# Attention plus gMLP on one core: attention output loaded four token tiles at a time, two raw weight blocks and one maxima row on other queues

## The chip, the cores and the metric

The kernel is one program on one core of a Trainium2 chip. The metric is the device time of one execution in microseconds (us), the median over the runs; a single execution is also recorded by the hardware profiler, and all views of the profile come from that one. In what follows TensorE is PE, its weight loads PEld, VectorE is DVE, ScalarE is ACT, GpSimd is POOL and SyncE is SP. SP computes nothing here: it issues transfers (DMAs), and a few are issued by ACT.

## The reference, cut to what matters

```python
def attention(x, wqkv, wo):                       # S 2048, D 640, 32 heads of 20, window 256
    q, k, v = split(x @ wqkv)
    scores = q @ k^T * 20 ** -0.5                 # key at most 255 tokens back, none ahead
    return (softmax(scores) @ v) @ wo

def gmlp(x, w_in, w_sp, b_sp, w_out):             # F 1728, half of it 864
    z = gelu(x @ w_in)
    z1, z2 = z[:, :864], layernorm(z[:, 864:])
    return (z1 * (w_sp @ z2 + b_sp)) @ w_out      # w_sp mixes the 2048 tokens

h = x + attention(layernorm(x), wqkv, wo)
h2 = h + gmlp(layernorm(h), w_in, w_sp, b_sp, w_out)
```

All is fp32. The two layernorms of 640 have no weights.

## The kernel before, in words

The 2048 tokens are 16 tiles of 128. A large product of fp32 operands is made of three: each operand is split into a high part (`hi`, a rounded copy, mostly made by ACT) and a low part (`lo`, the remainder, mostly made by DVE), and hi x hi, hi x lo and lo x hi are summed (`gemm`, line 98, is the loop for the output projection). Operands that DVE and ACT split are therefore always wanted by PE a little later.

**Stages.** Up to about 232 us come the first layernorm, the transposes and the projections to q, k and v; q and k are stored in DRAM (`qk_d`). From about 234 to 458 us runs attention. From 458 to about 525 us the attention output is multiplied by `wo`, and from 517 us on, mixed with its later tiles, z = h x w_in begins. The rest is the gMLP.

**Attention.** The heads are 8 groups of 4. A unit is one group and one tile of 128 keys, 128 units in all. The loop over s (line 823) does three things in each round. `max_item` works 16 units ahead: products of q and k for a running maximum per query (L344, then DVE's reduction L356). `score_item` makes the scores of unit s with the maximum already subtracted in the product (L410), takes the exponential on ACT (L413, four instructions of one head each per unit) and has POOL zero what lies outside the window (L415, L418); the result is a tile `pt`, of which there are four. `pv_item` multiplies the unit two rounds back by v (L438). Finished sums go through tiles `ot` to DRAM (`o_d`, L455), transposed: 32 rows per head, 20 of them values and the next the sum of the exponentials.

The maxima get into the score product as three extra rows of the operand in a group's slot: `max_rows` (L359 to L379) splits them in three on POOL, transposes them by a product, lets DVE copy them to `mt` (L376) and stores `mt` by DMA into rows 120 to 122 of the slot (L378). It does so twice per group, first for half 0 (b = 0), then for half 1 (b = 1, read from unit 8 of the group on). For group 0 the DMA is issued by ACT, for the other groups by SP. Rows of q and k for the next groups are loaded by SP (L311).

**The attention output's way back.** `load_o(j)` (L146 to L164) loads two tiles (256 tokens) into a ring of three buffers in `m1`: `load_tiles` issues five DMAs (L152), one for each chunk of 128 of the 640 rows, and one more brings the sums, each spread over the 20 rows of its head. For j = 0 the sums come straight from `o_d` and DVE takes their reciprocal over the whole buffer (L162). For the others they are read from `r_d` (`load_rs`, L158), where reciprocals already stand: `inverse_sums(c)` loads the sums of 512 tokens as a 128 x 128 tile `inv` (L389), some rounds later takes the reciprocal on DVE (L392) and has SP store it in `r_d` (L393). Tokens 512c and up are c, so r_d's second row block (c = 1) serves tiles 4 to 7.

For each tile `norm_o` (L168, DVE) multiplies by the reciprocals, `split_o` makes the two parts (`xb`; high by ACT or, at the start, by DVE L174, low by DVE L177), and `proj_o` runs the 30 products of L98. Then DVE adds x (tile `xh`, loaded by L144) and reduces, ACT squares and normalises, and the result goes to DRAM by ACT (L1537) and SP.

`load_win1` (L193, L194) loads two raw blocks of w_in, 442 KB each, into `wraw`. `win1_prep` (L937 to L962) turns w_in into the seven pieces `zl` with their parts, the high one by ACT (L897), the low one and the differences by DVE (L882). PE uses them at L1088.

**What sets the order.** Up to the end of attention (L859) the order of instructions on PE, ACT and DVE is that of the code, and so is SP's. Behind that, `wo_tile(i)` (from L1514) writes tile i's work together with three steps of `win1_prep` and, from tile 8 on, four steps of z, and a scheduler with its own model of times puts the instructions of each engine in order; each engine then runs its list strictly in that order. Before, `proj_early(s)` places by hand: x tiles 0 and 1 at s = 113, load 0 at 117, load 1 at 121, load 2 and the two raw blocks at 126, x tiles 2 and 3 and the last sums at 127. Loads 3 to 7 are called in `wo_tile` of tiles 0, 2, 4, 6 and 8.

In the function that follows these lines are the ones to find: L152, L158 and L162 (loads and first reciprocal), L168, L174, L177 (norm and split), L194 (raw blocks), L378 (maxima row).

Of the kernel before, what the change touches and what calls it, by code (L numbers as in the profile page):

```python
# [8 lines left out]
F32 = mybir.dt.float32  # L9
# [7 lines left out]
P = 128  # L17
S = 2048
D = 640
H = 32  # L20
DH = 20
NT = S // P
# [14 lines left out]
def block_kernel(ctx, tc, x, wqk, wv, wo, w_in, wsp, bsp, w_out, out):  # L37
# [66 lines left out]
    mem = {}  # L104

    def open_early(pl):
        mem["m1"] = pl.tile([P, 6 * D + 6 * P], F32, name="m1")
        mem["xh"] = [pl.tile([P, D], F32, name=f"xh{i}") for i in range(4)]
        mem["inv"] = [pl.tile([P, P], F32, name=f"inv{i}") for i in range(2)]
        mem["wraw"] = pl.tile([P, 2, 2, HF], F32, name="wraw")  # L110
# [23 lines left out]
    def m1(lo, *shape):  # L134
        return view(mem["m1"], lo, *shape)
# [9 lines left out]

    def load_o(j):  # L146

        t = slice(2 * j * P, (2 * j + 2) * P)
        ot, rs = m1(j % 3 * 2 * D, KD, 2 * P), m1(6 * D + j % 3 * 2 * P, 2 * P)
        def load_tiles():  # L150
            for k in range(KD):
                nc.sync.dma_start(ot[:, k], o_d[:, 4 * k:4 * k + 4, t])  # L152

        for i in range(2):
            ots[2 * j + i] = (ot[:, :, i * P:(i + 1) * P], rs[:, i * P:(i + 1) * P])

        def load_rs(base=r_d[:, t], step=S):
            nc.sync.dma_start(rs, bass.AP(tensor=base.tensor, offset=base.offset, ap=[[step, H], [0, 4], [1, 2 * P]]))  # L158

        def load_sums():  # L160
            load_rs(o_d[:, DH, t], 32 * S)
            return lambda: nc.vector.reciprocal(out=rs, in_=rs)  # L162

        return load_tiles, load_rs, load_sums  # L164

    def norm_o(i, eng):
        ot, rs = ots[i]
        eng.tensor_tensor(out=ot, in0=ot, in1=rs[:, None, :].to_broadcast([P, KD, P]), op=OP.mult)  # L168
# [22 lines left out]
            nc.vector.tensor_tensor(out=wo_part(1, k), in0=wo_raw(k), in1=wo_part(0, k).bitcast(F32), op=OP.subtract)  # L191

    def load_win1(b):  # L193
        nc.sync.dma_start(mem["wraw"][:, b], w_in[2 * b * P:(2 * b + 1) * P, :FH].rearrange("k (h c) -> k h c", h=2))  # L194

    def proj_early(s):

        k, odd = divmod(s - 98, 2)
        if 0 <= k < KD and not odd:
            nc.sync.dma_start(wo_raw(k), wo_d[k])  # L200
        if 111 <= s < 111 + 2 * KD:
            split_wo(s - 111)
        if s == 113:
            for i in range(2):
                load_x2(i)
        if s == 117:
            tiles, _, sums = load_o(0)
            mem["invert"] = sums()
            tiles()
        if s == 121:  # L210
            tiles, mem["rs"], _ = load_o(1)
            tiles()
            mem["invert"]()
        if s == 122:
            mem["rs"]()
            norm_o(0, nc.vector)
        if s == 123:
            split_o(0, True)
        if s == 124:
            norm_o(1, nc.vector)  # L220
        if s == 125:
            split_o(1, True)
        if s == 126:
            for b in range(2):
                load_win1(b)
            tiles, mem["rs"], _ = load_o(2)
            tiles()
        if s == 127:
            for i in (2, 3):
                load_x2(i)  # L230
            mem["rs"]()


    with ExitStack() as ab:
# [124 lines left out]
        def max_rows(g, b):  # L359


            n, cols, st = (40, 32)[b], m_cols.pop(b), slot_w[g % 3]
            m3 = tmp2.tile([P, 3, n], BF16, tag="m3", bufs=1, name=f"m3_{g}_{b}")
            mr = tmp2.tile([P, n], F32, tag="mr", bufs=1, name=f"mr{g}_{b}")
            nc.gpsimd.tensor_copy(out=m3[:, 0], in_=cols)
            nc.gpsimd.tensor_tensor(out=mr, in0=cols, in1=m3[:, 0], op=OP.subtract)
            nc.gpsimd.tensor_copy(out=m3[:, 1], in_=mr)
            nc.gpsimd.tensor_tensor(out=m3[:, 2], in0=mr, in1=m3[:, 1], op=OP.subtract)
            if b == 0:
                nc.gpsimd.tensor_copy(out=m_cols[1].rearrange("p (h r) -> p h r", h=4)[:, :, :2],  # L370
                                      in_=cols.rearrange("p (h r) -> p h r", h=4)[:, :, 8:])
            yield
            ps = s1_tile()[:3 * n, :P]
            nc.tensor.matmul(ps, m3.rearrange("p a c -> p (a c)"), minus, start=True, stop=True)
            mt = tmp2.tile([3 * n, P], BF16, tag="mt", bufs=1, name=f"mt{g}_{b}")
            nc.vector.tensor_copy(mt, ps)  # L376
            yield
            (nc.sync if g else nc.scalar).dma_start(st[b][0][120:123], mt.bitcast(F32))  # L378
            yield  # L379

        p_tiles, pv_tiles, inverse, put_later = {}, {}, [], []
# [1123 lines left out]
    def run(n):  # L1505
        for f in later.pop(n, []):
            f()
        if 0 <= n < len(steps):
            steps[n][0]()
            steps[n][1]()  # L1510
# [3 lines left out]
    def wo_tile(i):  # L1514
        if 1 < i + 1 < NT:
            split_o(i + 1, i == 1)
        if i % 2 == 0 and i + 6 < NT:
            for f in load_o(i // 2 + 3)[:2]:
                f()
        if i + 2 < NT:  # L1520
            norm_o(i + 2, nc.vector)
        for n in (4,) if i == 0 else (i + 4,) if i + 4 < NT else ():
            load_x2(n)
        if i < LAG:
            run(i - LAG)
        if i < 2:
            for _ in inverse[2 + i]:
                pass
        ps = pre_ps[i] if i < 2 else proj_o(i, acc_tile(i))
        xt = hs.pop(i)  # L1530
        h3 = xt.rearrange("p (a b) -> p a b", a=2)
        mv = const.tile([P, 5], F32, tag="mv", bufs=3, name=f"mvc{i}")
        nc.vector.tensor_tensor_reduce(out=h3, in0=ps[:, :, :HD], in1=h3, scale=1.0, scalar=0.0,
                                       op0=OP.add, op1=OP.add, accum_out=mv[:, 0:1])
        nc.vector.tensor_scalar(out=mv[:, 1:2], in0=mv[:, 0:1], scalar1=-1.0 / D, scalar2=None, op0=OP.mult)
        nc.scalar.activation(hn(i), xt, AF.Square, bias=mv[:, 1:2], accum_out=mv[:, 2:3])
        nc.scalar.dma_start(h_d[i], xt)  # L1537
        nc.vector.tensor_scalar(out=mv[:, 2:3], in0=mv[:, 2:3], scalar1=1.0 / D, scalar2=EPS, op0=OP.mult, op1=OP.add)
        nc.gpsimd.tensor_tensor(out=mv[:, 3:4], in0=mv[:, 2:3], in1=half, op=OP.pow)
        if i in (2, 5):  # L1540
            nc.vector.tensor_scalar(out=ones[:, i // 5:i // 5 + 1], in0=mv[:, 3:4], scalar1=1.0, scalar2=1.0,
                                    op0=OP.max, op1=OP.min)
        nc.vector.tensor_tensor(out=mv[:, 4:5], in0=mv[:, 1:2], in1=mv[:, 3:4], op=OP.mult)
        nc.scalar.activation(hn(i), xt, AF.Identity, scale=mv[:, 3:4], bias=mv[:, 4:5])
        store_hn(i)
        for _ in range(3):
            next(w1, None)
# [62 lines left out]
```

## Time and profile before

| | |
|---|---|
| median of 3 runs | 1094.03 us (1093.27 to 1096.68) |
| the profiled execution's own time | 1096.98 us |
| its span (first to last instruction) | 1095.3 us |
| mean granted PE clock | 0.993 |

Busy time by stage, from the windows of the profile, in us (in brackets the stage's length):

| stage | PE | DVE | ACT | POOL | clock | DMA share |
|---|---|---|---|---|---|---|
| to 232 (232.0) | 228.3 | 148.7 | 114.4 | 92.0 | 1.00 | 0.52 |
| attention, 232 to 458 (226.0) | 212.2 | 205.8 | 206.8 | 167.1 | 1.00 | 0.58 |
| output projection, 458 to 525 (67.0) | 59.7 | 53.4 | 35.2 | 9.3 | 0.90 | 0.80 |
| gMLP, 525 to the end (570.3) | 561.7 | 384.4 | 230.8 | 107.2 | 1.00 | 0.57 |

How to read the views: a row of the timeline begins with its start and its length in us; then come the engine, the line, the operation with what it writes and reads, and how many such instructions it holds; the bracket gives the idle time of the engine ahead of the row, and what ended it. ACTq and SPq are the parts of ACT and SP that issue transfers, and a row with DMA alone is the transfer itself, from its issue to its completion. A row of the windows gives its bounds and length, the busy time of each engine with the count of instructions in brackets, then the clock granted to PE (1.00 is full speed), the share of the 16 DMA engines that were busy, and GB/s.

### The profile page before, as it was taken

How to read it: one execution, taken by the hardware profiler on the slowest of the kernel's cores; microseconds unless marked ns; L12 is line 12 of the kernel's file. 1: busy time of each engine (PE TensorE's matmuls, PEld its weight loads, DVE VectorE, ACT ScalarE, POOL GpSimd, SP SyncE). 2: the span in 40 equal slices, each digit the busy share in tenths (PEclk: the TensorE clock that was granted, in tenths of full speed). 3: DMA queues.
4: the chain of work that ended last, by engine and by line, in shares of the span. 5: the costliest groups of instructions: out<-in, count | busy, mean ns of one | idle time of the engine just before them, and what ended most of it. 6: DMA issues, size and time to landing. Idle time of an engine off the chain costs nothing.

```text
span 1095.3 us, 27454 instructions
## 1 busy us (share of the span) xinstructions
PE 1061.9 (97%) x10457; PEld 954.0 (87%) x10457; DVE 792.2 (72%) x2133; ACT 587.2 (54%) x1221; POOL 375.6 (34%) x538
## 2 busy tenths in 40 slices
PE   9999999989999999988999999999999999999998
PEld 7998877657887787688999999899999989999998
DVE  7755852879999999678865777758656898676643
ACT  4446764348998999746755566534335532222210
POOL 3322454447776777701100056165342000000000
PEclk9999999999999999989999999999999999999999
DMA  6222567765666664487854621355585577766654
GB/s 217 66 82 78 168 199 255 246 219 180 195 214 189 207 187 128 147 289 256 289 180 142 221 84 51 111 205 188 176 298 202 182 246 231 237 223 194 184 159 123
DMA packets 114402, 203.96 MB, mean 186 GB/s; under 512 B 12149, under 2 KB 61189, under 8 KB 114181
## 3 DMA queue, kind: packets, MB, share of 16 engines
q1 hardware_dynamic: 109408, 188.21, 53.2%
q0 software_dynamic: 2336, 8.70, 2.2%
q10 hardware_dynamic: 2526, 5.30, 1.3%
q8 instruction: 82, 1.34, 0.5%
q14 instruction: 50, 0.41, 0.1%
HBM read 132.44 MB, written 70.92 MB: 186 GB/s over the span
## 4 chain that ended last, share of the span: by engine, by line
PE 70%; DMA 10%; DVE 9%; ACT 4%; issue 3%; SPq 2%; POOL 2%; ACTq 0%; DVEq 0%; POOLq 0%
PE bank_a L1336 20%; PE bank_b L1392 9%; PE bank L662 6%; PE pv L438 6%; PE bank L410 4%; PE bank L344 4%; PE wo_ps L98 2%; PE bank_a L1088 2%; DMA fx<-hn_d 2%; DVE zl L882 1%; PE bank_b L1088 1%; DVE row L882 1%; DVE aw L882 1%; DMA fx<-w_in_in 1%; DMA fx<-wsp_in 1%
## 5 line engine op out<-in xcount | busy, mean ns | idle before, releaser
L413 ACT ACTIVATE pt<-bank 128x384 f32<-128x384 f32 (+2 forms) x512 | 202.6, 496 | 17.6 <-PE bank L410 11.9
L1336 PE MATMUL bank_a<-zl,aw 128*128 128x432 f32 x759 | 167.9, 358 | 0.0
L356 DVE CUSTOM_DVE_ANT_0 junk<-bank,strip 128x288 bf16<-128x288 f32 x392 | 157.2, 453 | 9.2 <-PE bank L344 6.9
L888 ACT ACTIVATE aw<-fx 128x512 fp32r<-128x512 f32 (+3 forms) x147 | 84.9, 591 | 134.9 <-PE bank_a L1336 78.4
L1336 PEld LDWEIGHTS bank_a<-zl,aw 128*128 128x128 f32 x759 | 142.4, 188 | 6.1
L1336 PE MATMUL bank_a<-ze,aw 128*128 128x432 f32 x573 | 131.8, 359 | 3.3 <-ACT aw L888 1.2
L438 PE MATMUL pv<-pt,v_sb 128*32 128x192 f32 (+3 forms) x1984 | 125.7, 322 | 3.7 <-POOL pt L415 1.9
L1336 PEld LDWEIGHTS bank_a<-ze,aw 128*128 128x128 f32 x573 | 106.2, 188 | 10.0 <-ACT aw L888 2.1
L410 PE MATMUL bank<-slot 123*32 123x288 bf16 (+6 forms) x1536 | 106.7, 280 | 4.1 <-ACT pt L413 3.5
L882 DVE TENSOR_TENSOR aw<-fx,aw 128x512 fp32r<-128x512 f32 (+3 forms) x146 | 100.6, 702 | 12.8 <-ACT aw L888 12.6
L415 POOL TENSOR_SCALAR_AFFINE_SELECT pt<-pt 128x512 f32<-128x512 f32 x128 | 83.6, 654 | 53.0 <-ACT pt L413 52.6
L882 DVE TENSOR_TENSOR row<-bank_a,row 128x432 f32<-128x432 f32 x95 | 56.8, 600 | 54.3 <-PE bank_a L1336 35.8
L1141 PE MATMUL bank_a<-win,aw 128*128 128x432 f32 x480 | 95.3, 359 | 0.3 <-ACT row L888 0.3
L1141 PEld LDWEIGHTS bank_a<-win,aw 128*128 128x128 f32 x480 | 90.1, 188 | 4.6 <-ACT row L888 0.7
L344 PE MATMUL bank<-slot 120*32 120x288 bf16 (+2 forms) x1280 | 89.2, 282 | 3.4 <-DVE mcol L356 2.9
L1392 PE MATMUL bank_b<-wout,y_sp 128*128 128x320 f32 (+1 forms) x588 | 90.2, 309 | 0.2 <-ACT y_sp L139 0.2
L1392 PEld LDWEIGHTS bank_b<-wout,y_sp 128*128 128x128 f32 (+1 forms) x588 | 88.0, 188 | 0.9 <-ACT y_sp L139 0.5
L418 POOL TENSOR_SCALAR_AFFINE_SELECT pt<-pt 128x512 f32<-128x512 f32 x112 | 74.0, 661 | 0.0
L410 PEld LDWEIGHTS <-slot 123*32 123x32 bf16 x1536 | 52.6, 96 | 20.7 <-issue 9.3
L438 PEld LDWEIGHTS pv<-pt,v_sb 128*32 128x32 f32 x1984 | 58.8, 110 | 8.9 <-POOL pt L415 3.4
L356 DVE CUSTOM_DVE_ANT_0 junk<-bank,mask 128x384 bf16<-128x384 f32 (+2 forms) x120 | 50.7, 448 | 13.8 <-PE bank L348 10.1
L139 ACT ACTIVATE y_sp<-yt 128x896 fp32r<-128x896 f32 x14 | 13.3, 952 | 83.5 <-PE bank_b L1392 82.8
(243 smaller groups left out, 2221.7 us busy)
## 6 DMA issues: line engine op xcount, KB each, us to landing
fx<-wsp_in SPq DMA_DIRECT2D x30, 512.0 KB
slot<-qk_d SPq DMA_DIRECT2D x72, 200.0 KB
qk_d<-rest SPq DMA_DIRECT2D x32, 384.0 KB
slot<-qk_d SPq DMA_DIRECT2D x72, 160.0 KB
fx<-hn_d SPq DMA_DIRECT2D x32, 320.0 KB
o_d<-ot SPq DMA_DIRECT2D x64, 128.0 KB
z_d<-row SPq DMA_DIRECT2D x18, 432.0 KB
y_d<-z SPq DMA_DIRECT2D x16, 448.0 KB
```

The lines of the kernel that those rows point to most:

```text
L344: nc.tensor.matmul(ps[32 * j:32 * j + 32, :n], part(st, half, 120, 0, hh, q0, 32), part(st, half, 120, 1, hh, lo + skip * j, n), start=Tru ...
L356: nc.vector.tensor_tensor_reduce(out=junk[:, :n], in0=ps[:, :n], in1=keep, scale=1.0, scalar=NEG, op0=OP.add, op1=OP.max, accum_out=m_cols ...
L410: nc.tensor.matmul(ps[32 * i:32 * i + 32, b:e], part(st, half, 123, 1, hh, k0, 32), part(st, half, 123, 0, hh, kb * P + b, e - b), start=T ...
L413: nc.scalar.activation(pt[:, hh, :n], ps[:, :n], AF.Exp, scale=SCALE)
L415: nc.gpsimd.affine_select(out=pt[:, :, :P], in_=pt[:, :, :P], pattern=[[0, 4], [1, P]], base=0, channel_multiplier=-1, compare_op=OP.is_ge ...
L418: nc.gpsimd.affine_select(out=pt[:, :, 256:], in_=pt[:, :, 256:], pattern=[[0, 4], [-1, P]], base=-1, channel_multiplier=1, compare_op=OP. ...
L438: nc.tensor.matmul(ps[32 * hh:32 * hh + 32, a - 512 * c:b - 512 * c], v_sb[:, kb, v0:v0 + 32], pt[:, hh, a - kb * P:b - kb * P], start=fir ...
L882: (eng or nc.vector).tensor_tensor(out=out, in0=a, in1=b, op=op)
L888: nc.scalar.activation(out, a, AF.Copy)
L1141: nc.tensor.matmul(b[0][:, :HF], a[t][:, x, kk], win2[0][:, y, kk, h * HF:(h + 1) * HF], start=kk + x + y == 0, stop=kk == KD - 1 and x == 1)
L1336: nc.tensor.matmul(ps, w[m][x][:, k], zc[k][m][:, y], start=start and k + x + y == 0, stop=stop and k == 3 and x == 1, skip_group_check=True)
L1392: nc.tensor.matmul(ps[j][:, :HD], y[:w, a, k, :], e1["wout"][:w, b, k, j * HD:(j + 1) * HD], start=(k == 0 and a + b == 0), stop=(k == KF ...
```

## The change

Three things are changed, and `m1` grows from six tiles' room to eight.

First, `load_o` covers four tiles (512 tokens) with two buffers instead of two tiles with three. Load 0 stays at s = 117, load 1 moves from 121 to 124 with its sums at 127, and loads 2 and 3 are called in `wo_tile` of tiles 3 and 7. Second, `load_win1` is called in `wo_tile(0)` and issued by ACT, no more by SP at s = 126. Third, the maxima row of half 1 of group 0 is issued by SP instead of ACT.

```diff
-        mem["m1"] = pl.tile([P, 6 * D + 6 * P], F32, name="m1")
+        mem["m1"] = pl.tile([P, 8 * D + 8 * P], F32, name="m1")
...
-        t = slice(2 * j * P, (2 * j + 2) * P)
-        ot, rs = m1(j % 3 * 2 * D, KD, 2 * P), m1(6 * D + j % 3 * 2 * P, 2 * P)
+        t = slice(4 * j * P, (4 * j + 4) * P)
+        ot, rs = m1(j % 2 * 4 * D, KD, 4 * P), m1(8 * D + j % 2 * 4 * P, 4 * P)
...
-        for i in range(2):
-            ots[2 * j + i] = (ot[:, :, i * P:(i + 1) * P], rs[:, i * P:(i + 1) * P])
+        for i in range(4):
+            ots[4 * j + i] = (ot[:, :, i * P:(i + 1) * P], rs[:, i * P:(i + 1) * P])
...
-        nc.sync.dma_start(mem["wraw"][:, b], w_in[2 * b * P:(2 * b + 1) * P, :FH].rearrange("k (h c) -> k h c", h=2))
+        nc.scalar.dma_start(mem["wraw"][:, b], w_in[2 * b * P:(2 * b + 1) * P, :FH].rearrange("k (h c) -> k h c", h=2))
...
         if s == 121:
-            tiles, mem["rs"], _ = load_o(1)
-            tiles()
             mem["invert"]()
         if s == 122:
-            mem["rs"]()
             norm_o(0, nc.vector)
...
         if s == 124:
+            tiles, mem["rs"], _ = load_o(1)
+            tiles()
             norm_o(1, nc.vector)
...
-        if s == 126:
-            for b in range(2):
-                load_win1(b)
-            tiles, mem["rs"], _ = load_o(2)
-            tiles()
...
-            (nc.sync if g else nc.scalar).dma_start(st[b][0][120:123], mt.bitcast(F32))
+            (nc.sync if g or b else nc.scalar).dma_start(st[b][0][120:123], mt.bitcast(F32))
...
-        if i % 2 == 0 and i + 6 < NT:
-            for f in load_o(i // 2 + 3)[:2]:
+        if i in (3, 7):
+            for f in load_o(i // 4 + 2)[:2]:
                 f()
...
+        if i == 0:
+            for b in range(2):
+                load_win1(b)
```

How the instructions of the engines stand now is shown below, as lists in program order without times; a number at the end of a tile's name only tells tiles apart. Behind about line 226 the changed kernel's lines are 6 lower than before (L378 is L372, L389 is L383, L393 is L387, L455 is L449, L882 is L876), and in `wo_tile` 3 to 6 lower.

On ACT, in units 2 and 3 of attention (`pt_2374` is unit 2's tile, `pt_2436` unit 3's), the maxima row stood between the two units' exponentials:

```order
L413 ACTIVATE pt_2374<-bank_130 128x384
L413 ACTIVATE pt_2374<-bank_128 128x384
L413 ACTIVATE pt_2374<-bank_129 128x384
L378 DMA slot_1_106<-mt_1_2392 3x32x64
L413 ACTIVATE pt_2436<-bank_130 128x384
L413 ACTIVATE pt_2436<-bank_128 128x384
```

Now the exponentials there follow each other without it, and the row stands on SP, behind an x tile (`xh`) that is moved there too, among the stores of q and k and the loads of the next group:

```order
L590 DMA qk_d_65<-rest_147 128x3x256
L144 DMA xh_9552<-x_in 128x640
L372 DMA slot_1_106<-mt_1_2392 3x32x64
L311 DMA xb_100<-qk_d_62 20x4x640 x2
L311 DMA xb_100<-qk_d_63 20x4x512 x3
L449 DMA o_d<-ot_0_0_2599 128x256
```

So SP issues two DMAs more at this place than before, and the loads behind them come after the row.

On SP at the end of attention, before the change, the second store to `r_d` (that of `inv_8918`) stood behind the raw blocks and five loads of tiles:

```order
L152 DMA m_8912<-o_d 128x1x256 x2
L389 DMA inv_8917<-o_d 128x1x128
L194 DMA wraw<-w_in_in 128x864 x2
L152 DMA m_8912<-o_d 128x1x256 x5
L393 DMA r_d<-inv_8918 32x4x128
L144 DMA xh_8915<-x_in 128x640
L144 DMA xh_8916<-x_in 128x640
L158 DMA m_8912<-r_d 128x1x256
```

In the changed kernel the five loads of tiles 4 to 7 stand ahead of attention's last two stores, and the raw blocks are gone:

```order
L383 DMA inv_8918<-o_d 128x1x128
L152 DMA m_8912<-o_d 128x1x512 x5
L449 DMA o_d<-ot_2_0_9376 128x256
L449 DMA o_d<-ot_2_1_9379 128x256
L383 DMA inv_8917<-o_d 128x1x128
L387 DMA r_d<-inv_8918 32x4x128
L144 DMA xh_8915<-x_in 128x640
L144 DMA xh_8916<-x_in 128x640
L158 DMA m_8912<-r_d 128x1x512
```

The second store to `r_d` now follows the load of sums directly, and one read brings the reciprocals of four tiles instead of two.

On DVE, around tile 4's low part (`xb_101<-m_8912`, L177), four steps of `win1_prep` stood between the norms of two tiles (L168) before:

```order
L168 TENSOR_TENSOR m_8912<-m_8912 128x5x128 x2
L1535 TENSOR_SCALAR mvc_9623<-mvc_9623 128x1
L882 TENSOR_TENSOR zl_9570<-wraw,zl_9570 128x432
L882 TENSOR_TENSOR zl_9576<-wraw,zl_9576 128x432
L882 TENSOR_TENSOR wraw<-wraw 128x432
L882 TENSOR_TENSOR zl_9580<-wraw,zl_9580 128x432
L168 TENSOR_TENSOR m_8912<-m_8912 128x5x128 x2
L177 TENSOR_TENSOR xb_101<-m_8912,xb_101 128x640
```

Now the norms come first, a tile's reduction (L1530) and tile 4's low part follow, and the steps of `win1_prep` come behind:

```order
L168 TENSOR_TENSOR m_8912<-m_8912 128x5x128 x2
L1540 TENSOR_TENSOR mvc_9591<-mvc_9591 128x1
L168 TENSOR_TENSOR m_8912<-m_8912 128x5x128 x2
L1530 ISA xh_8914,mvc_9611<-wo_ps_9503,xh_8914 128x640
L1530 ISA mvc_9611 128x1
L177 TENSOR_TENSOR xb_101<-m_8912,xb_101 128x640
L876 TENSOR_TENSOR zl_9562<-wraw,zl_9562 128x432
```

The four steps of `win1_prep` that were between the two pairs of norms are therefore no longer ahead of tile 4's low part.

More of the change, by code (lines that the diff above doesn't have):

```diff
@@ L152, in load_tiles @@
                 nc.sync.dma_start(ot[:, k], o_d[:, 4 * k:4 * k + 4, t])
-        for i in range(2):
-            ots[2 * j + i] = (ot[:, :, i * P:(i + 1) * P], rs[:, i * P:(i + 1) * P])
+        for i in range(4):
+            ots[4 * j + i] = (ot[:, :, i * P:(i + 1) * P], rs[:, i * P:(i + 1) * P])
         def load_rs(base=r_d[:, t], step=S):
-            nc.sync.dma_start(rs, bass.AP(tensor=base.tensor, offset=base.offset, ap=[[step, H], [0, 4], [1, 2 * P]]))
+            nc.sync.dma_start(rs, bass.AP(tensor=base.tensor, offset=base.offset, ap=[[step, H], [0, 4], [1, 4 * P]]))
         def load_sums():
```

## The prediction

> **What bounds the kernel now.** I read the page first, then the waits, the chain that ended last, and from there the timelines and windows around the two stretches in which TensorE (PE) stood still.
>
> ```profile
> PE 1061.9 (97%) x10457; PEld 954.0 (87%) x10457; DVE 792.2 (72%) x2133; ACT 587.2 (54%) x1221; POOL 375.6 (34%) x538
> ...
> PE   9999999989999999988999999999999999999998
> ```
>
> PE is busy for 97% of the span of 1095.3 us, so what an edit can win is a stall of PE, and the half-speed clock that follows a long one. Both places that the change touches hold such a stall. The first lies at the start of attention; these rows are ACT's, SP's, the chain's and PE's, and three windows (busy time of PE, PEld, DVE, ACT, POOL, then granted clock, DMA share, GB/s).
>
> ```profile
> 234.03 5.14 ACT L413 ACTIVATE pt<-bank 128x384 f32<-128x384 f32 x12 [0.28 <-PE bank L410]
> 241.18 0.74 ACTq L378 DMA_DIRECT2D slot<-mt  x1
> 242.29 4.85 ACT L413 ACTIVATE pt<-bank 128x384 f32<-128x384 f32 x12 [3.11 <-issue]
> ...
> 237.59 0.29 DVE L376 CAST mt<-bank 96x128 bf16<-96x128 f32 x1
> ...
> 234.71 1.57 SPq L317 DMA_DIRECT2D xb<-qk_d  x2
> ...
> 234.71 6.39 DMA xb<-qk_d
> ...
> 242.83 0.31 PE L410 MATMUL bank<-slot 123*32 123x288 bf16 x4 [2.78 <-ACT pt L413]
> ...
> 242.80:245.00 2.20, 2.17 (x64) 1.88 (x67) 1.28 (x7) 2.20 (x6) 1.01 (x2) 1.00 0.67 248
> 245.00:250.00 5.00, 5.00 (x155) 4.30 (x148) 4.95 (x26) 5.00 (x15) 3.58 (x7) 1.00 0.19 54
> ```
>
> ACT ends its exponentials at 239.17, the row that it must store (mt) has been ready since 237.88, and yet the DMA issue (L378) starts only at 241.18. The transfer issued by SP at 234.71 completes at 234.71 + 6.39 = 241.10, and the chain leads from it to ACT: the issue had to wait for an older transfer, and the exponentials queue behind it. PE stands for 2.78 us. Its clock stays at 1.00, and ACT is busy without a gap afterwards, so the stage is paced by ACT and DVE and the loss isn't made good.
>
> The second place is the output projection of attention. PE's two stalls, and the clock behind each:
>
> ```profile
> 481.16 1.43 PE L98 MATMUL wo_ps<-xb,xb 128*128 128x320 f32 x4 [3.29 <-DVE xb L177]
> 517.64 0.73 PE L1088 MATMUL bank_b<-zl,aw 128*128 128x432 f32 x1 [3.86 <-ACT zl L897]
> ...
> 480.00:485.00 5.00, 3.84 (x14) 3.85 (x15) 5.00 (x12) 1.19 (x2) 0.85 (x1) 0.50 1.02 360
> 485.00:490.00 5.00, 5.00 (x31) 5.00 (x31) 4.82 (x12) 3.37 (x6) 0.00 (x0) 0.84 0.86 284
> ...
> 520.00:525.00 5.00, 5.00 (x18) 4.64 (x17) 4.79 (x15) 3.52 (x7) 2.23 (x1) 0.59 0.79 225
> ```
>
> The first stall costs 3.29 us and, at the clock of the two windows, 3.84 x 0.50 + 5.00 x 0.16 = 2.7 us: 6.0. The second costs 3.86, half of the 2.36 us from 517.64 to 520 and 5.00 x 0.41 after it, 3.2: together 7.1. What PE waited for first is tile 4's low part, and this is how it came late, on DVE and SP:
>
> ```profile
> 474.50 1.56 DVE L168 TENSOR_TENSOR m<-m 128x640 f32<-128x640 f32 x2 [5.13 <-DMA o_d<-ot]
> 478.81 1.56 DVE L168 TENSOR_TENSOR m<-m 128x640 f32<-128x640 f32 x2 [0.62 <-DMA m<-r_d]
> 480.28 0.82 DVE L177 TENSOR_TENSOR xb<-m,xb 128x640 fp32r<-128x640 f32 x1
> ...
> 461.34 0.51 SPq L389 DMA_DIRECT2D inv<-o_d  x1
> 461.91 1.06 SPq L194 DMA_DIRECT2D wraw<-w_in_in  x2
> 463.02 3.10 SPq L152 DMA_DIRECT2D m<-o_d  x5
> 466.22 0.57 SPq L393 DMA_DIRECT2D r_d<-inv  x1
> 466.83 1.82 SPq L144 DMA_DIRECT2D xh<-x_in  x2
> 471.08 0.52 SPq L158 DMA_DIRECT2D m<-r_d  x1
> ```
>
> The second reciprocal row (r_d) stands on SP behind the two raw blocks (1.06 us) and five loads (3.10 us), and then takes until 471.07 to land, with 884 KB of raw blocks ahead of it; only then is it read back, and DVE starts tile 4 at 474.50. (The profile names the store that landed last; by the code L168 needs the row issued at 471.08.) DVE, in its order, then waits once more for the sums of tiles 6 and 7 before it gets to tile 4's L177.
>
> **Part by part.** A. *The maxima row on SP.* ACT loses L378 and its wait; PE gains 2.78, by ACT's own gap 3.11. I take 2.78. On SP it stands behind tile 4's x (xh4), which is moved there too, and ahead of group 2's loads: SP gets two issues more (0.74 and about 0.4), and can wait for mt until 237.88; those loads are needed a whole group later. The row must land before half 1 is read at unit 8, eight units of four exponentials after 234.03: 8 x 4 x 0.41 (6.61 / 16, below) = 13.1, 247.2. Issued near 239, even 6.39 us of landing ends at 245.4; past 247.2 each us would be a us of PE.
>
> The Trainium skill ("DMA: Bandwidth & Descriptors", Issuing engines are not separate DMA queues) says that starting DMAs from another engine saves only the time to initiate them. By it this part would be worth the 0.74 of the issue; the trace's 3.11 disagrees, since the issue carried a wait.
>
> B. *Loads of four tiles, raw blocks off SP.* In numbers: 8 x 6 issues become 4 x 6.
>
> ```profile
> L152 SPq DMA_DIRECT2D m<-o_d x40: 512/602/1343, 444.7 to 511.4; - x40
> ...
> 447.55 1.74 DVE L162 RECIPROCAL m<-m 128x256 f32<-128x256 f32 x1
> 450.97 0.95 DVE L392 RECIPROCAL inv<-inv 128x128 f32<-128x128 f32 x1 [1.67 <-DMA inv<-o_d]
> 453.82 0.87 DVE L177 TENSOR_TENSOR xb<-m,xb 128x640 fp32r<-128x640 f32 x1
> 454.61 1.25 DVE L168 TENSOR_TENSOR m<-m 128x640 f32<-128x640 f32 x1
> 458.62 0.56 PE L98 MATMUL wo_ps<-xb 128*128 128x320 f32 x2
> ```
>
> SP saves 24 issues at 0.6, some 14 us, if one of 512 tokens issues as fast as one of 256 (the same 128 rows); the bytes stay the same. The new first load brings twice the bytes and its reciprocal twice the elements: 0.95 for 128 and 1.74 for 256 give about 3.3 for 512, 1.6 more, which the 1.67 of idle ahead of L392 takes up. DVE's new order puts two more norms (up to 1.25 each, beside POOL) and one more cast (about 0.8) ahead of tile 0's L177, which moves from an end at 454.7 to about 457.8. PE wants it at 458.62: hidden by 0.8 us of attention's tail, beyond which it costs us for us.
>
> Then the chain of tile 4. SP now has the second r_d store straight behind the third read of sums (461.34, which waits for stores that ACT makes). It needs the reciprocal of DVE at about 461.9, lands some 2.5 to 3.7 us later without the raw blocks, xh takes its 1.8 meanwhile, and the sums, issued at 465 to 466, land at 468 to 469.5, after 3 to 3.5 us as before (471.08 to 474.50). So DVE starts tile 4 at about 468.5 and, two norm pairs (3.1) and one tile's reduction and L177 (1.6) later, has it at 473; PE asks at 477.9 (481.16 less 3.29). The first stall goes, with its clock loss: 6.0.
>
> What is late next is the second stall. It hangs on the last w_in block (zl, L897), which DVE prepares, so DVE's work from tile 4's norm on sets it:
>
> ```profile
> 474.50:514.30 39.80, 35.98 (x220) 35.07 (x218) 35.95 (x81) 22.78 (x43) 4.67 (x6) 0.91 0.94 310
> ...
> 513.70 0.60 DVE L882 TENSOR_TENSOR row<-row,row 128x432 f32<-128x432 f32 x1
> ```
>
> DVE worked 35.95 of these 39.80 us. In its new order two more norms (1.6) stand in that stretch: 37.5. From 468.5 it ends at 506.0 without a gap and at 509.2 with the 3.2 of gaps that are left (3.85 less the 0.62 at 478.81), so 8.3 to 5.1 earlier than 514.3. PE comes 6.0 earlier and again waits some 3 to 5 us, so the clock falls as before. I take 6.5 us for the whole of B (the middle, a little less since the start at 468.5 may be 1.5 late); bounds 3.5 and 9.8.
>
> C. *Raw blocks issued by ACT.* In the new order they stand between the exponentials of units 111 and 112.
>
> ```profile
> 465.89 0.35 ACTq L1537 DMA_DIRECT2D h_d<-xh  x1
> ...
> 431.40 2.40 ACT L413 ACTIVATE pt<-bank 128x384 f32<-128x384 f32 x6 [0.26 <-PE bank L410]
> 436.71 1.65 ACT L413 ACTIVATE pt<-bank 128x384 f32<-128x384 f32 x4 [0.33 <-PE bank L410]
> 247.26 6.61 ACT L413 ACTIVATE pt<-bank 128x384 f32<-128x384 f32 x16
> ```
>
> Two issues cost ACT 0.7 (0.35 each) to 1.5 us (0.74 each). ACT's gaps there, 0.26 and 0.33, hide most of it. I take 0.3; bounds 0 and 1.5, and the exponentials behind them are what POOL and then PE wait for. Their bytes leave the stretch from 462 on, where DMA is full.
>
> Sum: 2.8 + 6.5 - 0.3 = 9.0 us. The profiled execution took 1096.98 us and becomes 1088.0; the median of the runs is 1094.03, 2.95 less, and becomes **1085.0**. Of the page's 40 slices of 27.4 us, PE's two below nine tenths here are 465 to 520; behind them it has nine in each but the last, so I expect the gain to last to the end.
>
> **Rivals.** *Both stalls go* (0.12). The gap of 2.78 left the clock at 1.00, those of 3.29 and 3.86 halved it. If DVE has no gaps and PE's second wait falls below that, its 3.86 and 3.2 go as well: 2.8 + 6.0 + 7.1 - 0.3 = 15.6, 1078.4. Against it: DVE paces that stretch. The Trainium skill ("TensorE: Matmul & The Clock Gate", Why this matters for your kernels) asks for no idle gaps above about 3 us; the trace agrees at these three.
>
> *The transfers bound it* (0.14). DMA is busy 0.94 at 310 GB/s from 474.5 to 514.3, and no byte is saved: the sums land as late as before whoever issues them. Then only A is left: 1094.0 - 2.8 = 1091.2. For it speaks the 1.02 of 480 to 485; against it that the raw blocks leave, and that SP, not the bytes, delayed r_d until 466.22. The Trainium skill's sentence under A would have it so.
>
> *Slower: the last loads hold DVE* (0.06). The loads of tiles 12 to 15 now stand on SP behind the store of tile 2's normalised row, which waits for ACT and so for DVE; DVE norms these four tiles in one block ahead of the w_in block that PE waits for. I put their landing at 497 to 500 and DVE there at about 502. Each us past that is a us of PE; from 11 us late (the 9.0, and the 2 of slack) the kernel is slower. At 15 late: 1094.0 - 9.0 + 13 = 1098.0.
>
> **How the numbers follow.** The forecast has 0.68. A measurement of this kernel can tell about 0.3%, 3.3 us, from no change. Forecast and both-stalls are faster: 0.80; transfers-bound is the same: 0.14; slower 0.06. The forecast's own bounds are 2.8 + 3.5 - 1.5 = 4.8 to 2.8 + 9.8 = 12.6, or 1081.4 to 1089.2. The range takes in the transfers rival at 1091.2 and on the other side reaches to 1079.0, leaving out about 0.18.
>
> **What would show it.** Right: no gap of ACT at L378's old place; tile 4's norm at least 4 us earlier against PE's first projection; no wait of PE for L177 there; one half-clock stretch in place of two, the rest of it before L1088. Wrong: tile 0's L177 after the end of attention's products; the norms of tiles 8 to 11 or 12 to 15 waiting for DMA; a wait of PE at unit 8; or stalls at new places after 525.

## The result, and the profile after

| | before | changed |
|---|---|---|
| median, runs of this comparison | 1095.36 us (4) | 1086.41 us (4) |
| ratio, 95% interval | | 0.9916 [0.9888, 0.9944] |
| the same, timed a second and a third time | 1093.98 and 1094.82 us | 1086.30 and 1085.30 us |
| their ratios | | 0.9925 [0.9904, 0.9945], 0.9919 [0.9902, 0.9935] |
| span of the profiled execution | 1095.3 us | 1082.5 us |

The changed kernel is 8 to 9 us faster, as forecast (9.0). The two spans differ by more, 12.8 us. The profiled execution of before was one of its longer ones and the first of the changed kernel one of its shorter ones (two more of it have spans of 1084.5 and 1082.2), so what the two traces differ by is read stage by stage below. Of the 12.8 us, 4.7 lie ahead of attention's last exponential, 3.0 between it and z's 22nd product (the one that waited 3.86; it starts at 517.64 before and at 509.93 now), and 5.1 behind that product. From there to the end the kernel before takes 577.7 us in its profile, the changed kernel 572.6 here and 574.0 and 574.2 in its later profiles, and the kernel with the row alone 575.8. So a part of those 5.1 us belongs to these two executions, and the 1.6 to 1.8 that are left against the row alone were not traced to a cause.

From the page of the changed kernel, busy time of the engines, and PE's busy tenths in 40 slices:

```profile
PE 1059.6 (98%) x10457; PEld 952.8 (88%) x10457; DVE 796.0 (74%) x2133; ACT 587.8 (54%) x1221; POOL 374.0 (35%) x538
...
PE   9999999999999999899999999999999999999998
```

PE does the same work in a shorter span; of the three slices below nine tenths ahead of the last one, one is left.

First place, the start of attention, ACT and SP of the changed kernel:

```profile
235.03 0.97 ACT L407 ACTIVATE pt<-bank 128x384 f32<-128x384 f32 x2 [0.27 <-PE bank L404]
236.16 3.51 ACT L407 ACTIVATE pt<-bank 128x384 f32<-128x384 f32 x8 [0.16 <-PE bank L404]
240.04 5.86 ACT L407 ACTIVATE pt<-bank 128x384 f32<-128x384 f32 x14 [0.36 <-PE bank L404]
...
239.72 0.77 SPq L372 DMA_DIRECT2D slot<-mt  x1
```

The gap of 3.11 behind the twelfth exponential is gone; the longest gap there is now 0.36, behind the tenth. The row is issued by SP at 239.72 and is in time: no wait of PE above 0.4 us follows at unit 8.

Second place, the output projection: PE's waits, and in a second piece the windows behind them (length, busy time of PE, PEld, DVE, ACT, POOL, clock, DMA share, GB/s):

```profile
479.86 0.56 PE L98 MATMUL wo_ps<-xb 128*128 128x320 f32 x2 [1.92 <-ACT xb L176]
481.38 0.90 PE L98 MATMUL wo_ps<-xb,xb 128*128 128x320 f32 x2 [0.66 <-DVE mvc L1532]
505.70 1.45 PE L1082 MATMUL bank_b<-zl,aw 128*128 128x432 f32 x6 [0.91 <-DVE mvc L1530]
```

```profile
480.00:485.00 5.00, 4.34 (x19) 4.08 (x20) 4.75 (x10) 1.81 (x4) 0.00 (x0) 0.66 1.02 353
500.00:505.00 5.00, 4.79 (x33) 4.53 (x31) 5.00 (x11) 2.44 (x6) 0.55 (x1) 1.00 1.02 342
505.00:510.00 5.00, 4.30 (x22) 4.12 (x23) 5.00 (x13) 3.99 (x8) 0.00 (x0) 1.00 0.40 130
```

The waits of 3.29 (for tile 4) and of 3.86 are gone. In their place stand 1.92 and 0.66, both at tile 5, and 0.91 at z's first product, and only the 1.92 is followed by a half-speed clock. DVE and SP on tile 4:

```profile
468.88 1.56 DVE L168 TENSOR_TENSOR m<-m 128x640 f32<-128x640 f32 x2 [2.40 <-DMA m<-r_d]
470.43 1.55 DVE L168 TENSOR_TENSOR m<-m 128x640 f32<-128x640 f32 x2
472.64 0.82 DVE L177 TENSOR_TENSOR xb<-m,xb 128x640 fp32r<-128x640 f32 x1
...
455.10 1.06 SPq L449 DMA_DIRECT2D o_d<-ot  x2
460.12 0.52 SPq L383 DMA_DIRECT2D inv<-o_d  x1
460.73 1.42 SPq L387 DMA_DIRECT2D r_d<-inv  x1
463.59 0.52 SPq L158 DMA_DIRECT2D m<-r_d  x1
```

Tile 4's norm starts at 468.88 instead of 474.50, almost as forecast (468.5). But attention's last exponential starts 4.7 us earlier too (452.50 instead of 457.21): against it the norm has moved from 17.3 to 16.4 us only (17.3 and 16.0 in the other two profiles of the changed kernel). So the forecast's number was met for another reason, and the experiments had to show what took the second wait away.

### The profile page after: what moved, and what is told of

It reads as the page before. It is cut to its first block, busy times and chain, and to the rows that moved or that the text cites. A ratio compares the mean times of both kernels' runs of the same rounds, so it can differ in the third digit from the quotient of the medians.

```text
span 1082.5 us, 27405 instructions
## 1 busy us (share of the span) xinstructions
PE 1059.6 (98%) x10457; PEld 952.8 (88%) x10457; DVE 796.0 (74%) x2133; ACT 587.8 (54%) x1221; POOL 374.0 (35%) x538
## 4 chain that ended last, share of the span: by engine, by line
PE 76%; DVE 10%; DMA 5%; ACT 4%; issue 2%; SPq 2%; POOL 1%; DVEq 0%; ACTq 0%; POOLq 0%
PE bank_a L1330 22%; PE bank_b L1386 9%; PE pv L432 6%; PE bank L404 4%; PE bank L338 4%; PE bank L656 4%; PE bank_a L1082 4%; PE wo_ps L98 4%; PE bank_b L1082 3%; PE bank_a L1135 2%; DVE zl L876 2%; ACT pt L407 1%; DVE row L876 1%; PE bank L537 1%; PE bank L535 1%
## 5 line engine op out<-in xcount | busy, mean ns | idle before, releaser
L407 ACT ACTIVATE pt<-bank 128x384 f32<-128x384 f32 (+2 forms) x512 | 202.1, 496 | 12.3 <-PE bank L404 8.2
L882 ACT ACTIVATE aw<-fx 128x512 fp32r<-128x512 f32 (+2 forms) x147 | 85.0, 592 | 138.8 <-PE bank_a L1330 74.0
L876 DVE TENSOR_TENSOR aw<-fx,aw 128x512 fp32r<-128x512 f32 (+2 forms) x146 | 100.9, 703 | 12.2 <-ACT aw L882 12.0
L876 DVE TENSOR_TENSOR row<-bank_a,row 128x432 f32<-128x432 f32 x95 | 56.9, 601 | 53.1 <-PE bank_a L1330 38.7
```

The lines of the kernel that those rows point to most:

```text
L407: nc.scalar.activation(pt[:, hh, :n], ps[:, :n], AF.Exp, scale=SCALE)
L876: (eng or nc.vector).tensor_tensor(out=out, in0=a, in1=b, op=op)
L882: nc.scalar.activation(out, a, AF.Copy)
```

## The experiments

Two parts of the change share one stage, so each was first done alone. The theories were these. The **chain theory** is the prediction's: what counts is when the second row of reciprocals is stored and read back. The **bytes theory** gives the gain to the 884 KB of raw blocks, the **issue-count theory** to SP's fewer issues. For the maxima row a **wait theory** stands against an **issue theory**. In us, a ratio is taken of 1094.

**The row alone.**

```diff
-            (nc.sync if g else nc.scalar).dma_start(st[b][0][120:123], mt.bitcast(F32))
+            (nc.sync if g or b else nc.scalar).dma_start(st[b][0][120:123], mt.bitcast(F32))
```

> The kernel before with one edit: the second maxima row of group 0 is issued by SP. Wait theory (the issue on ACT had to wait for an older transfer): ACT's gap of 3.11 us and PE's 2.78 there go, -2.8 us (2.3 to 3.3), ratio 0.9974; the output projection keeps both stalls (3.29 and 3.86). Issue theory (only the time to initiate the transfer is saved, 0.74): -0.7 us, ratio 0.9993. Rival that the row then lands late: a new PE wait at unit 8, near 247 us.

Measured: 0.9979 [0.9963, 0.9995], 2.3 us less (0.5 to 4.0). ACT's first 24 exponentials now run without a gap, while both waits of the output projection are still there, 2.78 and 3.60 instead of 3.29 and 3.86:

```profile
234.64 10.13 ACT L413 ACTIVATE pt<-bank 128x384 f32<-128x384 f32 x24 [0.28 <-PE bank L410]
...
477.38 1.43 PE L98 MATMUL wo_ps<-xb,xb 128*128 128x320 f32 x4 [2.78 <-DVE xb L177]
513.74 0.68 PE L1088 MATMUL bank_b<-zl,aw 128*128 128x432 f32 x1 [3.60 <-ACT zl L897]
```

The wait theory's 2.8 lies in the interval and the issue theory's 0.7 at its edge, so the next run separates them.

**The row on ACT's queue, two rounds later.**

```diff
-                if hh % 2 and u1 <= NU + 2 and u1 % NT in (2, 12):
+                if (hh % 2 and u1 <= NU + 2 and u1 % NT in (2, 12) and (u1, hh) != (NT + 2, 3)) or (u1, hh) == (NT + 4, 3):
```

> The kernel before with one edit: the second maxima row of group 0 stays on ACT's queue but is issued two rounds later, behind unit 4's exponentials, when the older transfer has completed. Wait theory: no wait is left, ACT pays only the issue of 0.74, PE's 2.78 goes, -1.5 to -2.5 us, nearly as much as on SP. Issue theory (what the row costs is its issue on ACT): 0. A wait that always lasts until the oldest transfers complete would show the same gap of 2 to 3 us, two units later.

Measured: 0.9981 [0.9969, 0.9994], 2.1 us less (0.7 to 3.4). ACT and its queue:

```profile
234.10 8.18 ACT L413 ACTIVATE pt<-bank 128x384 f32<-128x384 f32 x19 [0.27 <-PE bank L410]
242.09 0.78 ACTq L378 DMA_DIRECT2D slot<-mt  x1
242.17 0.48 ACT L413 ACTIVATE pt<-bank 128x384 f32<-128x384 f32 x1
```

The same issue on the same queue now stops nothing. The issue theory is out: the price was the wait for an older transfer, and the queue was the matter only as far as exponentials stood behind it. In the traces the DMAs take eight semaphores in turn, and in the kernel before, L378's is the one of the transfer issued at 234.71, which completed at 241.10.

**The raw blocks alone on ACT**, loads of two tiles as before.

```diff
-        nc.sync.dma_start(mem["wraw"][:, b], w_in[2 * b * P:(2 * b + 1) * P, :FH].rearrange("k (h c) -> k h c", h=2))
+        nc.scalar.dma_start(mem["wraw"][:, b], w_in[2 * b * P:(2 * b + 1) * P, :FH].rearrange("k (h c) -> k h c", h=2))
...
         if s == 126:
-            for b in range(2):
-                load_win1(b)
...
+        if i == 0:
+            for b in range(2):
+                load_win1(b)
```

> The kernel before with one edit: the two raw w_in blocks are issued by ACT in units 111 and 112, loads of two tiles as before. Chain theory (what counts is when the second row of reciprocals is stored and read back): the store still stands behind five loads of 0.6 us but no more behind 884 KB, so tile 4's norm starts 2 to 3 us earlier against PE's first projection and the gain is 3 to 5 us. Bytes theory (the 884 KB are all that matters): the whole of the output projection's gain, 6 to 7 us. Issue-count theory (SP's number of issues): about -1 us.

Measured: 0.9957 [0.9943, 0.9971], 4.7 us less (3.2 to 6.2). PE's waits:

```profile
479.24 1.43 PE L98 MATMUL wo_ps<-xb,xb 128*128 128x320 f32 x4 [4.21 <-DVE xb L177]
514.24 2.64 PE L1086 MATMUL bank_b<-zl,aw 128*128 128x432 f32 x10 [1.63 <-DVE zl L880]
```

The size is the chain theory's (the lower end of the bytes theory, 6, lies in the interval too), but not the place: the wait at tile 4, which the chain sets, is longer (4.21), and the one before z is shorter (1.63 instead of 3.86). Tile 4's norm starts 17.5 us after attention's last exponential (471.74 less 454.27), no earlier than before.

**The loads of four tiles alone**: the diff's edits of `load_o`, `m1`, `proj_early` and the calls in `wo_tile`, with the maxima row on ACT, the raw blocks on SP, and this in place of their new call:

```diff
+        if s == 126:
+            for b in range(2):
+                load_win1(b)
```

> The kernel before with one part of the change: loads of four tiles in two buffers, the raw blocks still issued by SP at round 126, the maxima row still on ACT. Chain theory: the store of the second reciprocal row is freed of the five loads but not of the raw blocks, so tile 4's norm starts 2 to 3 us earlier and the gain is 3 to 5 us. Issue-count theory: the whole gain of the output projection, 6 to 7 us. Bytes theory: about 0, both stalls stay.

Measured: 1.0021 [1.0007, 1.0034], 2.3 us **more** (0.8 to 3.7). PE's and DVE's rows:

```profile
475.45 3.03 DVE L168 TENSOR_TENSOR m<-m 128x640 f32<-128x640 f32 x4 [3.51 <-DMA o_d<-ot]
...
480.89 0.85 PE L98 MATMUL wo_ps<-xb,xb 128*128 128x320 f32 x4 [2.06 <-DVE xb L177]
513.43 2.50 PE L1085 MATMUL bank_b<-zl,aw 128*128 128x432 f32 x6 [6.46 <-DVE mvc L1535]
```

None of the three theories had this. The first wait shrinks to 2.06 and the one before z grows to 6.46: what is saved at tile 4 is paid before z, and more. The chain theory as it stood fell here.

**The changed kernel again.** No edit.

> The changed kernel once more. All theories: ratio 0.989 to 0.994 against before. If the profiled execution of the first run was merely a fast one, its span of 1082.5 becomes 1084 to 1086 and the part of the 12.8 us that lies behind 525 us shrinks; if the stalls set it, PE has again no gap above 2 us between 455 and 525 us.

Measured: 0.9925 [0.9904, 0.9945], span 1084.5; PE's one wait above 2 us between 455 and 525 us is 2.09, at tile 0. The sum of the three parts done alone is -2.3 - 4.7 + 2.3 = -4.7 us, the change has about -8.2: they don't seem to add up (the 3.5 us between them are about what the intervals leave open), and the question was whether the loads of four tiles are worth something once the raw blocks are away.

**The raw blocks on SP, but early**, where the changed kernel calls them:

```diff
-        nc.scalar.dma_start(mem["wraw"][:, b], w_in[2 * b * P:(2 * b + 1) * P, :FH].rearrange("k (h c) -> k h c", h=2))
+        nc.sync.dma_start(mem["wraw"][:, b], w_in[2 * b * P:(2 * b + 1) * P, :FH].rearrange("k (h c) -> k h c", h=2))
```

> The changed kernel with one line undone: the two raw blocks are issued by SP, but where the changed kernel calls them, so the order puts them on SP between the stores of group 6, some 30 us ahead of before's place. Place theory (what counts is that they are out of the way of the reciprocals at the end of attention): as the changed kernel, 0.990 to 0.994. Queue theory (they have to be on ACT): slower than the changed kernel by 1 to 3 us, 0.994 to 0.996.

Measured: 0.9945 [0.9924, 0.9965], 6.0 us less (3.8 to 8.3). The value lies in the range of the queue theory (0.994 to 0.996), not in that of the place theory, and is 2.2 us worse than the changed kernel's 0.9925, but the two intervals overlap. So it isn't settled whether ACT's queue is worth something of its own; if it is, the number for it, 2.2, is below the 4.7 between this place and that of the next run. In the trace PE waits 2.08 at tile 5, and the clock falls behind it (0.77 and 0.55 in the windows 480:485 and 485:490).

**The raw blocks on SP, behind the read of the reciprocals.** The line of the last experiment again, the call in `wo_tile(0)` taken out, and:

```diff
         if s == 127:
             for i in (2, 3):
                 load_x2(i)
             mem["rs"]()
+            for b in range(2):
+                load_win1(b)
```

> The changed kernel with the raw blocks on SP at round 127, behind the read of the second row of reciprocals: nothing is ahead of that row any more, but the raw blocks land last. Chain theory (tile 4's norm sets both stalls): tile 4's norm starts as in the changed kernel, 14 to 14.5 us after PE's first projection, and the time is within 2 us of it, 0.991 to 0.995. Raw theory (the gain comes from the raw blocks being there early, so that DVE has work while it waits): the stall before z stays at 4 to 6 us and the time is that of before or above, 0.998 to 1.003.

Measured: 0.9988 [0.9974, 1.0001], 1.3 us less (2.8 less to 0.1 more), so most of the gain is gone. The chain is as free as in the changed kernel (tile 4's norm starts 17.2 us after the last exponential, at 470.54), the wait before z is 2.19. The chain theory's time is missed. The raw theory's time is met, but not the wait of 4 to 6 before z that it needs. Where the rest went is shown in part only: a later wait of PE, on operands of the gMLP, that is 1.0 to 1.4 us in the other kernels is 2.71 here:

```profile
687.34 2.31 PE L1332 MATMUL bank_a<-ze,aw 128*128 128x432 f32 x6 [2.71 <-ACT row L884]
```

**The chain made earlier.** Three edits to the changed kernel:

```diff
-                if g == 7:
+                if g == 7 and c:
                     inverse.append(inverse_sums(c))
...
-            for _ in range(5 if c else 4):
+            for _ in range(3 if c == 1 else 5):
...
+            mem["rs"]()
             for i in (2, 3):
                 load_x2(i)
-            mem["rs"]()
...
-            for _ in inverse[2 + i]:
+            for _ in inverse[1 + i]:
```

> The changed kernel, with three edits on the chain of reciprocals: that of tiles 0 to 3 is dropped, since nothing reads it any more, the second reciprocal is taken two rounds earlier, so that its store stands on SP ahead of the wait for the stores of tiles 8 to 11, and the sums are read ahead of the two x tiles. Chain theory: the store is issued 3 us earlier against PE's first projection, tile 4's norm 3 to 5 us earlier, the 0.4 to 2.1 us that PE waits for tile 0 goes, and so do the 0.7 to 2.6 us around tile 4 to 6: 2 to 4 us faster than the changed kernel, 0.988 to 0.991. Work theory (DVE is busy without gaps from there on and sets the end of the stage whenever it starts): at most the reciprocal's 0.95 us of DVE, 0.991 to 0.993.

Measured: 0.9940 [0.9921, 0.9959], 6.6 us less than before, no better than the changed kernel. This was the chain theory's own test, and the chain did move: DVE starts tile 4's norm 12.3 us after the last exponential (466.56 less 454.23) instead of 16.0 to 17.3.

```profile
466.56 3.03 DVE L168 TENSOR_TENSOR m<-m 128x640 f32<-128x640 f32 x4 [0.76 <-DMA m<-r_d]
478.83 0.83 DVE L168 TENSOR_TENSOR m<-m 128x640 f32<-128x640 f32 x1 [1.88 <-DMA m<-r_d]
480.83 2.29 DVE L168 TENSOR_TENSOR m<-m 128x640 f32<-128x640 f32 x3
483.04 0.82 DVE L177 TENSOR_TENSOR xb<-m,xb 128x640 fp32r<-128x640 f32 x1
...
483.91 0.90 PE L98 MATMUL wo_ps<-xb,xb 128*128 128x320 f32 x2 [5.34 <-DVE xb L177]
```

The four microseconds came back as one wait: the order now has the norms of tiles 8 to 11 ahead of tile 5's low part, DVE waits 1.88 for their sums and works 3.1 us on them, and PE waits 5.34 for tile 5.

**The norms of tiles 8 to 15 on POOL**, in that kernel:

```diff
-            norm_o(i + 2, nc.vector)
+            norm_o(i + 2, nc.gpsimd if i > 5 else nc.vector)
```

> The kernel with the three edits on the chain of reciprocals, and the norms of tiles 8 to 15 on POOL instead of DVE. Order theory (there the norms of tiles 8 to 11 stood on DVE ahead of tile 5's low part and waited for their sums, which made PE's stall of 5.34): that stall goes, DVE has 6 us less to do, 3 to 6 us faster than the changed kernel, 0.987 to 0.990. Work theory turned round (POOL takes much longer for a norm than DVE's 0.78 and its power for the layernorm stands behind them): a new stall of the same size, 0.993 to 0.996.

Measured: 0.9960 [0.9943, 0.9977], clearly worse than the changed kernel on the same chip (0.9919 [0.9902, 0.9935]) and no better than the kernel it was made from, whose interval it overlaps. POOL, DVE and PE:

```profile
479.94 6.76 POOL L168 TENSOR_TENSOR m<-m 128x640 f32<-128x640 f32 x4 [3.15 <-DMA fx<-w_in_in]
486.66 0.54 POOL L1536 TENSOR_TENSOR mvc<-mvc,half 128x1 f32<-128x1 f32 x1
...
487.24 0.15 DVE L1538 TENSOR_SCALAR ones<-mvc 128x1 f32<-128x1 f32 x1 [3.44 <-POOL mvc L1536]
...
490.67 0.70 PE L98 MATMUL wo_ps<-xb,xb 128*128 128x320 f32 x2 [2.66 <-ACT xb L176]
493.19 1.44 PE L98 MATMUL wo_ps<-xb,xb 128*128 128x320 f32 x4 [1.29 <-DVE xb L177]
```

The wait of 5.34 is gone, as it should be if it came from these norms. In its place four norms on POOL (1.7 us each here, 0.76 on DVE) hold up a layernorm's power, DVE waits 3.44 for that, and PE 2.66 and 1.29.

**The change without the loads of four tiles**: the maxima row on SP and the raw blocks on ACT, the diffs of the first and third experiment together.

> The kernel before with two of the three parts: the maxima row on SP and the raw blocks on ACT, loads of two tiles as before. Additive theory (the row's 2.0 to 2.3 us and the raw blocks' 4.7 add up, and loads of four tiles bring little of their own): -6.5 to -7 us, 0.9935 to 0.994, within 2 us of the changed kernel. Loads theory (the four-tile loads are what makes the stall before z vanish): -3 to -5 us, 0.9955 to 0.997, and a stall of more than 2 us before z.

Measured: 0.9926 [0.9912, 0.9941], on the same chip as the changed kernel's 0.9919 [0.9902, 0.9935]. The additive theory holds, a little on the better side (8.1 us; the two alone make 7.0). On top of the row the raw blocks bring 5.8 here. The loads of four tiles add 0.8 us, which these intervals cannot tell from nothing. PE's longest wait in the stage is here:

```profile
476.09 0.85 PE L98 MATMUL wo_ps<-xb,xb 128*128 128x320 f32 x4 [1.89 <-DVE mvc L1539]
```

**Without the first chain of reciprocals**, the first of the three edits on the chain alone (the first and the last of the four pieces shown there).

> The changed kernel without the chain of reciprocals of tiles 0 to 3 (its load of sums, reciprocal and store), whose result nothing reads any more. Tile 0 theory (DVE waits 2.2 to 3.9 us for that load ahead of tile 0's norm, and so PE starts the projection late): PE's first projection comes 0.8 us after attention's last exponential instead of 1.9 to 3.2, and the kernel is 1 to 2.5 us faster than the changed one, about 0.990 to 0.9915. Cover theory (a later wait takes it back): as the changed kernel, 0.992 to 0.993.

Measured: 0.9913 [0.9897, 0.9930], 0.7 us better than the changed kernel beside it and not to be told from it. In the trace the wait at tile 0 goes as the tile 0 theory has it: PE's first projection starts 1.4 us after the last exponential (the 0.8 of the expectation was too low), as before the change, instead of 1.9 to 3.2. But the time shows little of it.

**The changed kernel a third time.** No edit.

> The changed kernel a third time, to stand beside the others on the same chip: 0.990 to 0.994 by all theories.

Measured: 0.9919 [0.9902, 0.9935].

**What DVE had to do.** For this stage the account that fits best is one of DVE. The rows are the stretch from the start of attention's last exponential to z's 22nd product (L1088 of before, the one that waited 3.86), one of the kernel before, one without the loads of four tiles, one with these alone, and one of the changed kernel (its third profile); columns as in the windows above.

```profile
457.21:517.64 60.43, 52.64 (x354) 50.72 (x346) 47.08 (x103) 29.64 (x58) 7.11 (x9) 0.94 0.82 270
```

```profile
452.15:509.70 57.55, 53.73 (x353) 51.29 (x346) 45.79 (x101) 29.28 (x56) 5.99 (x8) 0.94 0.83 268
```

```profile
457.20:519.39 62.19, 52.62 (x353) 50.18 (x354) 53.64 (x117) 33.73 (x64) 8.95 (x10) 0.95 0.82 271
```

```profile
451.37:508.02 56.65, 51.94 (x353) 49.98 (x346) 51.29 (x108) 29.73 (x58) 7.74 (x8) 0.97 0.83 276
```

Length less busy time is DVE's idle time: 13.4 us before, 11.8 without the loads of four tiles, 8.6 with these alone, 5.4 in the changed kernel (7.5 and 6.7 in its first and second profile, over 57.4 and 58.1 us). The loads of four tiles take 4.2 to 6.4 us of waiting from DVE, but put 4.1 to 6.6 us more work (norms and casts of later tiles, steps of w_in) ahead of that product: they about cancel. Taking the raw blocks out of the way leaves the work about as it is (45.8 and 47.1), and the stretch is 2.9 us shorter. That this is a matter of DVE's order rather than of the amount alone is what the two runs on the chain point to; it was not tried to give DVE another order by hand. Moving the raw blocks' call also changed the order that the scheduler gives DVE: in the kernel without the loads of four tiles, three steps of `win1_prep` and a tile's reduction stand between the two pairs of norms, where four steps stood. So the runs show that the raw blocks' new place brings the gain, but not how much of it comes from the early bytes and how much from the new order. Nor does the stage hold all of the time: the kernel with the chain made earlier has 57.5 us here, as the changed kernel, and is by its number some 2 us slower (the intervals overlap).

## Why the prediction was right, and where its steps were not

**A, the row (2.78).** Right within the intervals: 2.3 and, on ACT but later, 2.1. The transfer was in time. The Trainium skill ("DMA: Bandwidth & Descriptors", Issuing engines are not separate DMA queues) counts only the time to initiate; here that was 0.78 on ACT's own queue with the stall gone, and the wait ahead of it was the rest.

**B, loads and raw blocks (6.5).** The sum was right: 8.2 to 9.2 in all, less 2.3, leaves 5.9 to 6.9. The way to it was not, so that the number came out right is in part luck. Its step "The first stall goes, with its clock loss: 6.0" failed. It rested on tile 4's norm coming 6 us earlier; against attention's last exponential it came 0.0 to 1.3 earlier, and against PE's first projection 1.4 (14.5 instead of 15.9), where I had asked for at least 4. Two terms were mis-sized. I left the third load of sums at its old place, 4.1 us behind that exponential (461.34 less 457.21). It came 7.6 us behind it: SP stood from 456.16 to 460.12 ahead of it (L383), behind the stores issued at 455.10. So the store followed at 460.73 and the read of the reciprocals at 463.59, 11.1 us behind the exponential instead of 7.8 to 8.8. And I let that read take 3 to 3.5 us "as before". With four tiles in it, 5.3 us passed from its issue to the norm (463.59 to 468.88; 5.2 and 6.1 in the other two profiles, 3.4 for two tiles before). And the step "hidden by 0.8 us of attention's tail" failed: DVE waited 2.22 for the first chain's sums (3.66 in the third profile), and PE began late at tile 0, in the third profile like this:

```profile
449.37 0.95 DVE L386 RECIPROCAL inv<-inv 128x128 f32<-128x128 f32 x1 [3.66 <-DMA inv<-o_d]
...
454.57 0.54 PE L98 MATMUL wo_ps<-xb 128*128 128x320 f32 x2 [2.09 <-issue]
```

The step "PE ... again waits some 3 to 5 us, so the clock falls as before" failed in the other direction: that wait is 0.91 and the clock stays. The term that was mis-sized is DVE's idle time in the stage. I left it 3.2 us of gaps behind tile 4's norm; the changed kernel has 0.4 to 0.7 there.

So B's two halves were exchanged: PE no longer waits for tile 4, but most of the first stall came back at tile 0 or tile 5, while the second went. The credit within B was wrong as well. I gave it to the freed store on SP, to which the loads of four tiles belong; by the runs the raw blocks make it, and the loads of four tiles nothing that can be measured.

**C, the issues on ACT (0.3).** Too small to be seen: from the first to the last exponential the kernel with row and raw blocks takes 217.7 us, that with the row alone 218.7, so there is no sign of a cost, but the three profiles of the changed kernel differ by 1.1 us there (217.5 to 218.6).

**The rivals.** "Both stalls go" is what the waits look like afterwards, at less than its price (15.6): the wait at tile 0, the 1.92 and one half-speed stretch were not in it. "The transfers bound it" is out as to the time, since the raw blocks alone, at unchanged bytes, brought 4.7; but its premise, that the sums land as late as before, is nearly what the traces show, against attention's end. "Slower: the last loads hold DVE": the loads of tiles 12 to 15 were in time, DVE taking their norms at 501.08 without a wait; the part that is slower alone, the loads of four tiles, is so by the wait before z.

## What to carry to other kernels

A DMA on a compute engine's queue is priced by the wait that it may carry, not by its issue time: look in the trace for the older transfer whose completion ends the gap, and either issue later or from a queue with nothing urgent behind it. When a stage's operands come from one in-order engine, a chain that feeds it can be made 4 us earlier and win nothing, because the engine's order decides which wait it turns into; add up that engine's busy and idle time up to the operand that PE waits for. A part of a change that looks like its main part should be run alone, and left out alone: here the largest edit of the three was worth nothing that could be measured.

## What the runs showed of the hardware that was not expected

The half-speed clock does not follow the length of PE's gap alone. The windows behind a gap of 2.09 us (454.57, third profile of the changed kernel) and behind one of 2.06 (480.89, loads of four tiles alone):

```profile
455.00:460.00 5.00, 4.41 (x20) 4.15 (x19) 4.81 (x7) 0.00 (x0) 0.00 (x0) 0.66 0.65 203
```

```profile
480.00:485.00 5.00, 4.11 (x28) 4.11 (x29) 5.00 (x12) 2.87 (x6) 1.25 (x1) 1.00 1.01 321
```

The first halves the clock for a part of the window, the second does not, nor did the 2.78 of before at the start of attention; the 1.92 of the changed kernel does. The prediction took the three gaps of before to mark a limit near 3 us, and the gap of about 3 us that the Trainium skill names ("TensorE: Matmul & The Clock Gate", Why this matters for your kernels) is not a limit that these runs confirm. At the start of attention the changed kernel even has a half-speed stretch with no gap of PE above 0.8 us ahead of it:

```profile
235.00:240.00 5.00, 4.79 (x97) 3.52 (x100) 4.47 (x26) 4.48 (x10) 4.21 (x9) 0.66 0.79 263
```

In the clock records of all these profiles, every half-speed stretch between 10 us after the start and 10 us before the end lasts 3.41 or 6.83 us.

The norm of a tile, a multiply of 128x640 fp32 elements, took 0.76 us on DVE and, in the run with norms on POOL, 1.7 and 1.95 us there (means of two blocks of four).
